# Turning operands on TensorE by halves of 64 rows, and log sums in quarters of the array, in a fused gated recurrence and mixer

## The chip, the core and the metric

The kernel runs on one core of a Trainium2 chip. The metric is device time in microseconds, the median of several executions: 465.51 us for the kernel before the change, from 465.46 to 466.96 over 3 runs. The core has TensorE (matrix products into the eight accumulation banks, PSUM), VectorE, ScalarE, GpSimd, and SyncE, whose queue starts the loads and stores here. In the profile these are PE (with PEld for its weight loads), DVE, ACT, POOL and SP.

## The reference

All data is float32. First a gated linear recurrence is run for each of 4 batches and 8 heads, over 768 time steps with 48 channels; then a mixer works on each batch, a matrix of 768 times by 384 (8 heads of 48).

```python
f = 1.0 / (1.0 + np.exp(-f_logit))
state = np.zeros((B, H, D, D))
for t in range(S):
    state = f[:, :, t, :, None] * state + np.einsum('bhd,bhe->bhde', k[:, :, t], v[:, :, t])
    y[:, :, t] = np.einsum('bhd,bhde->bhe', q[:, :, t], state)
...
h = xt @ U @ V                       # xt: (batch, 384, 768); U: 768 x 32; V: 32 x 768
u = x + h.transpose(0, 2, 1)
out = u + np.maximum(u @ w_ch1, 0.0) @ w_ch2     # 384 -> 1536 -> 384
```

The weights of the mixer arrive as 64-bit floats, and the kernel turns them into 32-bit ones itself.

## The kernel before

**Units.** The recurrence is done in units: one unit is a pair of heads of one batch, so there are 16 units, 4 for each batch. In a unit the 768 steps are 12 chunks of 64 steps (`C = 64`, `NCH = 12`), or 6 blocks of 128 (`NBL = 6`). The channels of the two heads lie on the 128 partitions, each padded from 48 to 64. Inside a chunk the recurrence becomes matrix products: with X, the inverse of the product of the gates from the chunk's end back, and Y, the product from the start on, the scores are (k X)ᵀ (q Y), masked to be causal; between chunks a state of 48 by 48 is carried by a scan.

**Operands.** Loads bring f, k and q with time on the partitions (`nat`), while the products need the channels there (`T["k"]`, which is `kz`, and `T["q"]`, which is `qT`). So TensorE turns each block of 128 times by 128 channels against an identity matrix (`on_tensor`, line 777; for q in units 1 to 3 line 793). VectorE then multiplies the turned block with X or Y, from PSUM into SBUF (lines 799 and 796). Units 0 to 5 do it like this (`TURNED = 6`); later units are turned by VectorE and are not touched.

**Log sums.** In units 0 to 3 X and Y come from logarithms. ScalarE computes log(1 + exp(-f)) (lines 818, 820 and 825). TensorE multiplies each block with a triangular matrix, `later`, 128 by 130: two triangles of 64 on its diagonal, zeros elsewhere, and two more columns that give the sum over each chunk (`log_sums`, line 835). Such a float32 product runs as two passes, a turn as one. ScalarE takes exp of both signs (X and Y, lines 852 and 854), of the whole-chunk sums (`least`, line 856), copies those into a small tile (`wholes`, line 857) and spreads that over the 48 channels for the scan (`whole`, line 1012). Units 4 and 5 use a sigmoid and scans instead (`gates`, `keep`, `read`).

**The rest of a unit.** `scores` (line 975) and `mask` (line 988, VectorE, into `A`), `kept` (line 1002: k turned back, by halves of 64 rows already; then ScalarE's copy `kb`), `states` (line 1026: the increment `ds` of the state; then ScalarE's copy `added`), `scan` (line 1051, VectorE), `read` (line 1069: q times the old state), `inner` (line 1087: the masked scores times v; then ScalarE's copy into `x`). `scores`, `read`, `inner` and `states` already work on 64 rows and 64 columns of the array at a time.

**Order.** For batch 0 and the first mixer the order of every engine is written by hand, by the order of the calls (from line 1180 on). Each engine takes its instructions strictly in that order. In batch 0 nothing but the four units runs, and a unit's front (loads, logs, k, q of unit n + 1) is interleaved with the rear of unit n. VectorE unpacks the loaded k and q of unit n + 1 (line 808) ahead of unit n's scan. SyncE's queue holds the loads of units 0 to 3, U and V, the first weights, and then the loads of units 4 and on. The weights are converted by ScalarE (lines 91 and 92), VectorE (lines 98 to 100) and GpSimd (line 101) through two buffers `w_y`; U and V come at the end of batch 0, ahead of and between the work of unit 3.

Behind batch 0 the mixer of batch 0 starts: `x` is multiplied with U and V, the result is added, x is turned (line 288, by halves of 64 rows), and the first product with `w_ch1` runs (`ch1`, lines 300 and 318, 128 by 128 weights and 256 columns). Units 4 to 7 are interleaved with it, so that each operand of units 4 and 5 is turned between groups of that product. Behind it come the second product (line 355) and the next batches in the same manner, up to the last mixers, which run without units beside them.

**PSUM.** Two pools: `ps_big`, three tiles of two banks, and `ps_mm`, two tiles of one bank. The 128 by 384 matmuls named `idle` (`busy`, line 1190) run at the start, when TensorE has nothing to do yet; one more of 128 columns stands in unit 0.

## Time and profile before

| What | us |
|---|---|
| median of the 3 runs (lowest, highest) | 465.51 (465.46, 466.96) |
| span of the profiled execution, first to last instruction | 463.2 |
| TensorE busy | 455.2 |
| VectorE busy | 351.4 |
| ScalarE busy | 170.4 |
| GpSimd busy | 48.5 |
| batch 0, its four units, up to the mixer's first long group of products | 0 to 47.4 |
| units 4 and 5 turned, between the mixer's products | 55 to 89 |

The page gives no time of the profiled execution other than its span, which is 2.3 us shorter than the median of the runs. The page lists the busy time of each engine, a chain of work followed back from the last instruction, groups of instructions by line, and the loads. A busy TensorE is not TensorE at its best: matmuls overlap, and their ends are modelled. So for TensorE the distance from one group's start to the next one's is the better measure; the chain of waits gives that as a length. A count of matmuls in the profile is a count of passes.

### The profile page before, as it was taken

Reading aid. Unit: us, or ns where it says so; the run is one execution under the profiler, and the core shown is the slowest. Engines: PE = TensorE matmul, PEld = TensorE weight load, DVE = VectorE, ACT = ScalarE, POOL = GpSimd, SP = SyncE. Lnnn points to the kernel's source line nnn. Section 1 sums busy time; section 2 is a strip of 40 time slices with the busy share of each in tenths; the row PEclk is TensorE's granted clock in tenths of the full one; section 3 lists DMA queues with packets and bytes.
Section 4 is the critical chain, followed back from the end, with each engine's and each line's share of the span. In section 5 each row is a group of like instructions: output and inputs, shape, how many; then the busy total and the mean of one; then the engine's idle time right before and its main releaser. Section 6 shows DMA issues by size and latency. Waiting matters only on the chain.

```text
span 463.2 us, 13016 instructions
## 1 busy us (share of the span) xinstructions
PE 455.2 (98%) x5639; PEld 394.5 (85%) x5639; DVE 351.4 (76%) x585; ACT 170.4 (37%) x323; POOL 48.5 (10%) x56
## 2 busy tenths in 40 slices
PE   8999999999999999999999999999999999999997
PEld 5886888875666578999898888899989999999996
DVE  6778788979999677676765559977797887858652
ACT  6785776562333143323322323451412311212200
POOL 2002445634112001010000000000000000000000
PEclk9999999999999999999999999999999999999999
DMA  9959997577777604504633030100000000000001
GB/s 194 186 139 212 227 217 180 150 119 103 124 113 118 107 18 53 78 1 89 77 52 74 14 61 4 28 3 21 18 1 1 35 1 23 13 1 35 1 36 39
DMA packets 148583, 34.35 MB, mean 74 GB/s; under 512 B 136934, under 2 KB 146982, under 8 KB 148518
## 3 DMA queue, kind: packets, MB, share of 16 engines
q1 hardware_dynamic: 147718, 33.29, 37.1%
q8 instruction: 46, 0.75, 0.7%
q10 hardware_dynamic: 800, 0.15, 0.2%
q14 instruction: 19, 0.16, 0.1%
HBM read 28.70 MB, written 4.72 MB: 72 GB/s over the span
## 4 chain that ended last, share of the span: by engine, by line
PE 80%; DVE 11%; ACT 3%; DMA 2%; issue 2%; SPq 2%; DVEq 0%; ACTq 0%
PE pw L389 27%; PE pz L300 21%; PE pp L495 12%; PE po L355 5%; PE y L1069 2%; PE sc L975 2%; PE ds L1026 2%; PE y L1087 2%; PE pt L1002 1%; SPq L661 1%; DVE late L894 1%; PE pt L777 1%; DVE late L876 1%; PE pt L835 1%; DMA other<-in_f_logit_dram 1%
## 5 line engine op out<-in xcount | busy, mean ns | idle before, releaser
L300 PE MATMUL pz<-uT,w 128*128 128x256 f32 x492 | 111.5, 382 | 0.3
L300 PEld LDWEIGHTS pz<-uT,w 128*128 128x128 f32 x492 | 91.7, 190 | 12.9 <-ACT uT L289 0.6
L389 PE MATMUL pw<-zw,w_raw 128*128 128x192 f32 x216 | 38.0, 329 | 0.0
L389 PE MATMUL pw<-w,z_all 128*128 128x192 f32 x216 | 37.3, 327 | 0.0
L335 ACT ACTIVATE z_all<-pz 128x512 f32<-128x512 f32 x33 | 19.6, 598 | 45.1 <-PE pz L300 44.7
L389 PEld LDWEIGHTS pw<-w,z_all 128*128 128x128 f32 x216 | 35.3, 190 | 0.5
L389 PEld LDWEIGHTS pw<-zw,w_raw 128*128 128x128 f32 x216 | 35.1, 190 | 0.6 <-issue 0.3
L101 POOL TENSOR_TENSOR w<-w_y,w_r 128x384 int32<-128x384 int32 x24 | 31.5, 1311 | 37.0 <-DVE w_y L100 22.5
L876 DVE TENSOR_TENSOR_SCAN late<-fz,late 128x768 f32<-128x768 f32 x12 | 21.1, 1755 | 9.4 <-ACT fz L871 9.3
L488 ACT ACTIVATE other<-other 128x512 f32<-128x512 f32 x18 | 11.3, 630 | 40.3 <-DVE other L204 40.3
L355 PE MATMUL po<-w,zw 128*128 128x384 f32 x72 | 25.2, 495 | 0.0
L355 PE MATMUL po<-w,z_all 128*128 128x384 f32 x72 | 24.7, 493 | 0.0
L1057 POOL COPY st<-added 128x576 f32<-128x576 f32 x8 | 12.4, 1556 | 113.8 <-DVE added L1051 113.8
L988 DVE TENSOR_TENSOR A<-sc,causal 128x768 f32<-128x768 f32 x16 | 15.2, 953 | 8.5 <-PE sc L975 8.5
L355 PEld LDWEIGHTS po<-w,zw 128*128 128x128 f32 x72 | 13.2, 190 | 9.6 <-issue 0.8
L894 DVE TENSOR_TENSOR_SCAN late<-fz,other 128x768 f32<-128x768 f32 x12 | 21.0, 1750 | 0.2
L355 PEld LDWEIGHTS po<-w,z_all 128*128 128x128 f32 x72 | 13.3, 190 | 8.9 <-DVE o L204 0.6
L488 ACT ACTIVATE z_all<-z_all 128x512 f32<-128x512 f32 x12 | 7.6, 631 | 34.1 <-DVE z_all L204 34.1
L1034 ACT COPY added<-ds 48x576 f32<-48x576 f32 (+2 forms) x29 | 17.8, 619 | 4.5 <-PE ds L1026 4.1
L495 PE MATMUL pp<-v_nat,late 128*128 128x128 f32 x152 | 19.1, 275 | 0.0
L1069 PEld LDWEIGHTS y<-st,qT 48*64 48x64 f32 x704 | 13.6, 137 | 6.2 <-issue 4.5
L98 DVE TENSOR_SCALAR w_y<-w_y 128x384 f32<-128x384 f32 (+3 forms) x27 | 12.1, 449 | 8.8 <-ACT w_y L91 8.8
(233 smaller groups left out, 872.1 us busy)
## 6 DMA issues: line engine op xcount, KB each, us to landing
w_raw<-in_moe_w_ch_dram SPq DMA_DIRECT2D x18, 384.0 KB, 3.6
out_dram<-o SPq DMA_DIRECT2D x17, 192.0 KB, 1.9
v_nat<-in_v_dram SPq DMA_DIRECT2D x16, 144.0 KB, 3.8
v_nat<-in_v_dram SPq DMA_DIRECT2D x32, 72.0 KB, 3.5
zw<-in_moe_w_ch_dram SPq DMA_DIRECT2D x6, 384.0 KB, 5.1
out_dram<-o SPq DMA_DIRECT2D x14, 96.0 KB, 2.2
w<-in_k_dram SPq DMA_DIRECT2D x4, 288.0 KB, 4.1
w<-in_q_dram SPq DMA_DIRECT2D x4, 288.0 KB, 4.2
```

The costliest lines, as they stand in the source:

```text
L101: nc.gpsimd.tensor_tensor(dst.bitcast(I32), shaped(y.bitcast(I32)), shaped(r), ALU.add)
L300: nc.tensor.matmul(pm[:, i * 2 * P : (i + 1) * 2 * P], lhsT=w1[:, m, o : o + P], rhs=uT[a][:, m, :], start=(m == 0), stop=(m == NDC - 1))
L335: nc.scalar.activation(z[a, c][:, k : k + 2, :].rearrange("p i t -> p (i t)"), pm, AF.Relu)
L355: nc.tensor.matmul(pm, lhsT=z[a, i // NI][:, i % NI, s * P : (s + 1) * P], rhs=w2[:, i, :], start=(i == 0), stop=(i == NFC - 1))
L389: nc.tensor.matmul(W["pm"][:, n * HM : (n + 1) * HM], lhsT=lhs[:, i, :], rhs=rhs[:, i, :], start=(i == 0), stop=(i == NI - 1))
L488: nc.scalar.activation(dst, dst, AF.Relu, scale=float(SIGNS[n]))
L495: nc.tensor.matmul(pm[:, i, r * P : (r + 1) * P], lhsT=room["w"](wn)[:, r * P : (r + 1) * P], rhs=x_node(a, xn), start=((xn, wn) == of[0]) ...
L876: nc.vector.tensor_tensor_scan(backwards(X, S - 1, S), backwards(f, S, S), backwards(ends, S - 1, S), 0.0, ALU.mult, ALU.add,)
L894: nc.vector.tensor_tensor_scan(Y, f[:, 0:S], starts, 0.0, ALU.mult, ALU.add)
L988: nc.vector.tensor_tensor(T["A"], sc[:, :, 0 : NBL * C].rearrange("p h (c i) -> p h c i", i=C), causal.unsqueeze(1).unsqueeze(1).broadcast ...
L1034: nc.scalar.copy(added[r, 1:].rearrange("p (e c s) -> p e c s", c=NBL, s=2)[:, e], ds[r, :, 0 : NBL * D].rearrange("p s (c e) -> p e c s", ...
L1069: nc.tensor.matmul(o(c % 2, par, c // 2), lhsT=T["q"][rows[par], chunk[c]], rhs=T["st"][rows[par], c, :], start=(c <= 2), stop=False, skip ...
```

## The change

1. **Turning by halves.** `on_tensor` (f, k and q of units 0 to 5) and the turn of q in units 0 to 3 take blocks of 64 times by 128 channels: 12 instead of 6 for an operand. The upper and the lower 64 rows go to two different PSUM banks. The turn of q in unit 0 takes two tiles of `ps_mm`, as units 1 to 3 did.
2. **Log sums in quarters.** `later` shrinks to 128 by 65: the triangle of 64 and one column of ones, once for the upper and once for the lower rows. Each block's product becomes four of 64 rows by 64 columns of the array, 65 columns wide, 24 in all instead of 6. In unit 0 the two halves of the blocks go to two tiles of `ps_big`.
3. **Around it.** The views of X, Y, k and q run over halves, then blocks, in place of blocks by threes. The copy of the chunk sums (`wholes`) falls away in units 0 to 3: `spread` reads `least` directly. `whole` becomes a fixed tile whose first column is set once. The `idle` matmul of 128 columns in unit 0 is gone, and so are four small memsets on VectorE at the start and one on GpSimd.

```diff
-    later = const.tile([P, P + 2], F32, name="later")
-    nc.vector.memset(later, 0.0)
+    later = const.tile([P, C + 1], F32, name="later")
+    nc.vector.memset(later, 1.0)
     for s in range(2):
-        half = later[s * C : (s + 1) * C, s * C : (s + 1) * C]
-        nc.vector.memset(half, 1.0)
-        nc.vector.memset(later[s * C : (s + 1) * C, P + s : P + s + 1], 1.0)
+        half = later[s * C : (s + 1) * C, 0:C]
...
         def on_tensor(nm):
 
             pt = ps_big.tile([P, 2, 512], F32, name="pt", tag="big")
+            turn_by_halves(nm, [pt[:, s] for s in range(2)])
+            return pt[:, :, 0 : G * C].rearrange("p s (c t) -> p s c t", t=C)
+
+        def turn_by_halves(nm, pts):
             for c in range(NBL):
-                nc.tensor.transpose(
-                    pt[:, 2 * c // NBL, c % (NBL // 2) * P : (c % (NBL // 2) + 1) * P],
-                    nat[n % 2][nm][:, c].rearrange("p h d -> p (h d)"), ident,
-                )
-            return pt[:, :, 0 : G * C].rearrange("p a (c t) -> p a c t", t=C)
+                for s in range(2):
+                    g = slice(s * C, (s + 1) * C)
+                    nc.tensor.transpose(pts[s][:, c * C : (c + 1) * C],
+                                        nat[n % 2][nm][g, c].rearrange("p h d -> p (h d)"), ident[g, g])
...
-            if nm == "q" and 0 < n < HP:
-                for a in range(2):
-                    pt = ps_mm.tile([P, 512], F32, name="pq", tag="mm")
...
+            if nm == "q" and n < HP:
+                pts = [ps_mm.tile([P, 512], F32, name="pq", tag="mm") for _ in range(2)]
+                turn_by_halves(nm, pts)
+                for s, pt in enumerate(pts):
...
         def log_sums():
...
+            n_of = NBL // 2 if n == 0 else NBL
+            T["sums"] = []
+            for c0 in range(0, NBL, n_of):
+                pt = ps_big.tile([P, 2, 512], F32, name="pt", tag="big")
+                for c in range(n_of):
+                    for i in range(2):
+                        for par in range(2):
+                            k = i ^ par
+                            nc.tensor.matmul(
+                                pt[par * PAD : (par + 1) * PAD, k, c * (C + 1) : (c + 1) * (C + 1)],
+                                lhsT=nat[n % 2]["f"][k * C : (k + 1) * C, c0 + c, par, :],
+                                rhs=later[k * C : (k + 1) * C, :], start=True, stop=True,
+                            )
...
-            nc.scalar.copy(wholes[n % 2][:, 1:NCH], least[:, n, 1:NCH])
+            T["wholes"] = least[:, n, :]
...
         def spread():
-            whole = T["whole"] = one.tile([P, D, NCH], F32, name="whole")
-            nc.scalar.copy(whole, wholes[n % 2].unsqueeze(1).broadcast_to((P, D, NCH)))
+            nc.scalar.copy(whole[:, :, 1:], T["wholes"][:, 1:].unsqueeze(1).broadcast_to((P, D, NCH - 1)))
...
-                pieces += [lambda: busy(1, P)] + front(1, "gates", "gates_end") + rear(0, "scores", "mask")
+                pieces += front(1, "gates", "gates_end") + rear(0, "scores", "mask")
```

On TensorE one period of batch 0, from the increment `ds` of unit 1 to that of unit 2, stands like this before the change (`pt<-later` are the log sums, `pt<-ident,late` k turned, `pq` q turned, `pt<-ident,kz` k turned back; the shape is that of one output):

```order
L1026 MATMUL ds<-v_nat,kb 64x48 x24
L835 MATMUL pt<-later,late 128x130 x6
L975 MATMUL sc<-qT,kz_131 64x64 x24
L777 MATMUL pt<-ident,late 128x128 x6
L1069 MATMUL y<-st,qT 64x48 x22
L793 MATMUL pq<-ident,late 128x128 x6
L1002 MATMUL pt<-ident,kz_130 128x64 x12
L1087 MATMUL y<-v_nat,A 64x48 x24
```

The same period of the changed kernel:

```order
L1022 MATMUL ds<-v_nat,kb 64x48 x24
L834 MATMUL pt<-later,late 64x65 x24
L972 MATMUL sc<-qT,kz_127 64x64 x24
L781 MATMUL pt<-ident,late 128x64 x12
L1065 MATMUL y<-st,qT 64x48 x22
L781 MATMUL pq<-ident,late 128x64 x12
L999 MATMUL pt<-ident,kz_126 128x64 x12
L1083 MATMUL y<-v_nat,A 64x48 x24
```

No group has moved; three of the eight have more and smaller matmuls, and none of the period uses the whole array any more.

VectorE at the end of batch 0 in the changed kernel, from the unpacking of unit 3's k and q (`other<-w_90`) to the conversion of U; the scan is unit 2's:

```order
L806 COPY other<-w_90 128x12x48 x2
L1047 SCALAR_TENSOR_TENSOR st<-added,whole 128x576
L985 TENSOR_TENSOR A<-sc,causal 128x768
L797 TENSOR_TENSOR kz_127<-pt,late 128x768
L98 TENSOR_SCALAR w_y<-w_y 128x192
L99 TENSOR_SCALAR w_y<-w_y 128x192
L100 SCALAR_TENSOR_TENSOR w_y<-w_raw,w_y 128x192
L795 TENSOR_TENSOR qT<-pq,fz_125 128x384 x2
```

Before the change the same place reads (with the old line numbers):

```order
L808 COPY other<-w_90 128x12x48 x2
L1051 SCALAR_TENSOR_TENSOR st<-added,whole 128x576
L988 TENSOR_TENSOR A<-sc,causal 128x768
L799 TENSOR_TENSOR kz_131<-pt,late 128x768
L98 TENSOR_SCALAR w_y<-w_y 128x192
L99 TENSOR_SCALAR w_y<-w_y 128x192
L100 SCALAR_TENSOR_TENSOR w_y<-w_raw,w_y 128x192
L796 TENSOR_TENSOR qT<-pq,fz_129 128x128x3 x2
```

The order is the same; only the two multiplications of q run over halves of 64 times in place of blocks by threes. SyncE's loads stand in the same order before and after. On the mixer's side, each `L777 ... 128x128 x6` between groups of `L300` of units 4 and 5 has become `L781 ... 128x64 x12` at the same place.

## The prediction

> **What bounds the kernel now.** I read the page first, then the chain of waits in order of time, then the waits of each engine, and last the timelines of VectorE, ScalarE and SyncE where the chain leaves TensorE.

> ```profile
> PE 455.2 (98%) x5639; PEld 394.5 (85%) x5639; DVE 351.4 (76%) x585; ACT 170.4 (37%) x323; POOL 48.5 (10%) x56
> ```

> TensorE is busy 455.2 us of the span of 463.2, so at first sight every microsecond taken from it counts. The page has no time of the profiled execution beside this span; the median of the runs is 465.5 us, 2.3 us more. I work out a difference in the span and take it off the median.

> The change touches two stretches. In the first, the four units of batch 0, the chain runs along TensorE, unit after unit:

> ```profile
> 18.22 1.54 PE pt L835 x12
> 19.75 0.86 PE sc L975 x48
> 20.61 0.81 PE pt L777 x6
> ...
> 21.43 1.24 PE y L1069 x41
> 22.67 0.81 PE pq L793 x6
> 23.48 0.54 PE pt L1002 x12
> ...
> 24.89 0.92 PE ds L1026 x48
> ```

> Columns: start, length, engine and line, count. This is one unit: log sums (6 matmuls in two passes each), scores, k turned, old state read, q turned, k turned back. Only L1002 already goes by 64 rows: its 12 half blocks take 0.54, where 6 whole blocks take 0.81. But the next engine is close behind, as a window of one unit's length shows (length, then busy of PE, PEld, DVE, ACT, POOL):

> ```profile
> 15.80:23.40 7.60, 7.54 (x225) 6.57 (x224) 5.52 (x9) 6.24 (x14) 0.00 (x0) 1.00 0.94 213
> ```

> ScalarE has 6.24 of 7.60 us, VectorE 5.52, and the share of the DMA engines is 0.94. The second stretch, units 4 and 5, lies in 55 to 89 us, between the mixer's matmuls:

> ```profile
> 67.08 0.66 PE pt L777 x6
> 67.73 2.59 PE pz L300 x12
> 70.33 0.52 PE pt L1002 x12
> 70.84 2.79 PE pz L300 x12
> ```

> **The change, step by step: batch 0 on TensorE.** Each k or q turned by halves goes from 0.81 to L1002's 0.54: 0.27 less, twice a unit. The log sums become 24 matmuls, 48 passes, of 64 rows, 64 columns and 65 moving columns, on four quarters. No row has that shape. Nearest are the scores, also 48 passes on quarters with 64 moving columns (48 rows):

> ```profile
> 185.48 0.71 PE sc L975 x48
> 186.19 0.52 PE pt L1002 x12
> ```

> Here, with half-array work behind them, they take 0.71, and 0.86 above where whole-array work follows. For the log sums I take 0.80; the bounds are 0.71 and the 1.54 of now (no overlap gained). So they give 0.74, the two turns 0.54, the scores 0.15: 1.4 us of TensorE per unit.

> [...]

> **What of it reaches the end of batch 0.** Unit 0 gives nothing: its kz stands on VectorE behind the unpacking of its q, which waits for the load until 6.72:

> ```profile
> 6.72 0.46 DVE L808 COPY late<-w 128x576 f32<-128x576 f32 x1 [0.53 <-DMA w<-in_q_dram]
> ```

> Unit 1's log sums start when ScalarE's second half of the logs is done, as now:

> ```profile
> 11.66 1.61 PE L835 MATMUL pt<-later,other 128*128 128x130 f32 x12 [0.23 <-ACT other L825]
> ```

> From there ScalarE goes 0.7 earlier, and unit 1's `ds` (the matmuls of the state's increment) with it. Unit 2 adds its 0.74 and 0.15, so its `ds` (24.89) comes about 1.6 earlier. The copies of L857 (0.20 each on ScalarE) that fall away are part of what lets ScalarE follow. Then VectorE meets a load:

> ```profile
> 25.05 0.46 DVE L808 COPY other<-w 128x576 f32<-128x576 f32 x1 [0.76 <-DMA w<-in_k_dram]
> 26.19 0.46 DVE L808 COPY other<-w 128x576 f32<-128x576 f32 x1 [0.69 <-DMA w<-in_q_dram]
> 26.57 1.35 DVE L1051 TENSOR_TENSOR_SCAN st<-added,whole 128x576 f32<-128x576 f32 x1
> 28.56 0.96 DVE L988 TENSOR_TENSOR A<-sc,causal 128x768 f32<-128x768 f32 x1 [0.64 <-PE sc L975]
> 29.44 0.95 DVE L799 TENSOR_TENSOR kz<-pt,late 128x768 f32<-128x768 f32 x1
> ...
> 31.53 1.04 DVE L796 TENSOR_TENSOR qT<-pq,fz 128x384 f32<-128x384 f32 x2 [0.29 <-PE pq L793]
> ...
> 34.13 1.41 DVE L1051 TENSOR_TENSOR_SCAN st<-added,whole 128x288 f32<-128x288 f32 x2 [0.85 <-ACT added L1034]
> ```

> VectorE takes its work in order, and the unpacking of unit 3's k and q (L808) stands ahead of unit 2's scan, before and after. q lands at 26.19. Today that wait costs nothing, since the scan's input `added` comes from ScalarE at 26.51 (25.87 + 0.64 below). After the change it is there 1.6 earlier, and the scan still starts at 26.57. Will q land earlier? SyncE issues it from a queue with no pause:

> ```profile
> 20.34 0.55 SPq L640 DMA_DIRECT2D w<-in_k_dram  x1
> 20.93 0.47 SPq L640 DMA_DIRECT2D w<-in_q_dram  x1
> ```

> SyncE's waits name no compute engine between 17 and 20 us, the order of loads is the same after the change, and the DMA share is 0.94. I take the landing as fixed; the bounds are 0.4 later and, if TensorE or ScalarE do gate it, early enough not to bind.

> So at 26.57 everything gained so far is gone on VectorE, and what comes back is the idle time behind it. The scan ends at 27.92. The mask A follows at once instead of at 28.56, so kz of unit 3 is 0.64 earlier and ends at 29.75; TensorE, ahead by then, waits for the scan, reads the state (1.24), turns q (0.54) and turns k back at 29.8 instead of 31.30, 1.5 earlier. The conversion of U (L98 to L100, left out above) is 0.64 earlier too, and the wait of 0.29 for pq goes. ScalarE and GpSimd at this place:

> ```profile
> 25.87 0.64 ACT L1034 COPY added<-ds 128x576 f32<-128x576 f32 x1
> ...
> 31.39 0.59 POOL L101 TENSOR_TENSOR U<-w_y,w_r 128x192 int32<-128x192 int32 x1 [27.29 <-DVE w_y L100]
> ...
> 31.86 0.80 ACT L1006 COPY kb<-pt 128x768 f32<-128x768 f32 x1 [0.72 <-PE pt L1002]
> 32.56 0.32 ACT L91 ACTIVATE w_y<-w_raw 64x128 f32<-64x128 f32 x1
> ...
> 33.70 0.70 ACT L1034 COPY added<-ds 128x288 f32<-128x288 f32 x2
> ```

> The L91 at 32.56 writes the buffer (one of two) that GpSimd's add for U reads until 31.39 + 0.59 = 31.98; that becomes 31.34, so this L91 moves 1.2, not 1.5, and `added` and the last scan (34.13, whose 0.85 of idle covers it) move 1.2 with it. From that scan to 41.9 us the chain runs on VectorE almost without idle and hands this on to the mixer's start at 47.4. **Batch 0 gives 1.2 us**; bounds 0 and 2.7. The 2.7 is what arrives if no load binds: 1.6 up to `ds` of unit 2, and 0.74 + 0.15 + 0.27 of unit 3's log sums, scores and k.

> **Units 4 and 5.** Here whole-array matmuls of the mixer stand on both sides. Six whole blocks take 0.66 with 2.59 behind them; the half blocks of L1002 take 0.52, but the 12 passes of L300 behind them take 2.79 instead of 2.59. Together 3.25 against 3.31: **each turn by halves loses 0.06**, where a view of L1002 alone promises 0.14. Five of the six (f, k, q, f, k) come before 86 us: 0.3 lost. This part is PE's own path:

> ```profile
> 47.40:86.20 38.80, 38.80 (x249) 33.84 (x248) 33.90 (x60) 27.11 (x53) 18.39 (x16) 1.00 0.87 202
> 86.20:134.10 47.90, 47.11 (x775) 33.21 (x775) 42.65 (x59) 21.00 (x41) 15.38 (x10) 1.00 0.75 119
> ```

> [...]

> From 86 to 134 us the chain runs along VectorE (42.65 of 47.90 busy) and the loads that it frees, and TensorE then waits:

> ```profile
> PE pt L1002 <- DVE kz L805: 0.2, 1, 0.2
> ```

> That chain begins at a matmul's end at 86.2, so it moves as a whole with TensorE; the sixth turn (0.06) has this 0.2 as cover. Behind 134 us nothing changes.

> Removed memsets, the idle matmul of unit 0 and the narrower copy into `whole` lie beside waits: nothing, at most 0.1 each way. **Sum: 1.2 - 0.3 = 0.9 us less, 464.6 us** (span 462.3).

> **Rivals.**
> - *No load binds.* TensorE's gain of batch 0 passes on: 2.7 - 0.3 = 2.4, 463.1 us. For it: TensorE at 98%. Against it: the 0.69 wait for q at 26.19, with the scan 0.08 behind it.
> - *The gain is given back.* The loop of weight conversion and loads from 47 to 134 us, VectorE 33.90 of 38.80 and then 42.65 of 47.90 busy, does not start earlier, and only the six dearer turns stay: 465.5, at worst 465.9. Against it: its head hangs on TensorE and ScalarE, with waits between 47 and 86.
> - *The clock drops: slower.* TensorE's first matmuls, at the kernel's start, run at half rate although the clock column says 1.00:

> ```profile
> 1.07 4.09 PE L1190 MATMUL idle<-late 128*128 128x384 f32 x6 [1.07 <-DVE late L667]
> ...
> 98.62 4.03 PE L355 MATMUL po<-w,z_all 128*128 128x384 f32 x12
> ```

> Six passes of 384 columns take 4.09 there, twelve take 4.03 later. After the change TensorE idles about 1.7 us before 28 us, waiting for the scan, longer than any wait now (the longest is 1.1, at the start). If that is enough to slow it, 4.1 us of its work run at half rate and cost 2.05, just where it is on the path: 464.6 + 2.1 = 466.7. [...]

> **How the numbers follow.** Forecast (0.3 to 1.4 less) 0.58; no load binds 0.19; given back 0.17; clock 0.06. A measurement tells about 0.3%, 1.4 us, from no change. The forecast lies inside that. Faster by more: the first rival and the forecast's edge, 0.22; slower by more: part of the clock rival and worse drains, 0.06; same 0.72. The range goes from 463.0 (no load binds) to 466.0 (given back at its worst, 465.9) and leaves out the clock rival and the thin ends.

> **What would show it.** Right: log sums of 48 passes near 0.8 us and turns near 0.54 in batch 0; VectorE still waiting for q at 26.2, now with TensorE idle until the scan ends near 28; the first L300 group near 46.2 instead of 47.4; twelve passes of L300 at 2.8 behind every turn of units 4 and 5. Wrong: a scan of unit 2 well before 26.5, log sums above 1.0, or the six turns saving time.

## The result, and the profile after

The changed kernel takes **477.75 us**, the median of 4 runs (476.85 to 478.32), against 466.07 for the kernel before on the same chip (465.46 to 466.96): a ratio of 1.0247, 95% interval 1.0227 to 1.0267. (The ratios in this document are estimates, each with its interval, and not the quotients of the medians.) The forecast was 464.6, its range 463.0 to 466.0. The profiled execution has a span of 475.1 us, 11.9 more than before.

The page of the changed kernel, first the busy time of TensorE, then the queue that carries instructions (packets, MB, share):

```profile
PE 458.7 (97%) x5865; PEld 395.1 (83%) x5865; DVE 350.6 (74%) x582; ACT 169.6 (36%) x319; POOL 48.5 (10%) x55
...
q8 instruction: 48, 0.79, 0.7%
```

TensorE is busy 3.5 us longer, though the groups were to get shorter. The second line will matter: 0.79 MB in 48 packets are 16.4 KB each, for 2 x 5865 weight loads and matmuls about 245 instructions to a packet.

The chain of waits in time (start, length, what) shows where the time goes:

```profile
11.36 0.73 PE pt L834 x33
12.10 2.11 issue
14.21 0.46 PE pt L834 x15
14.67 0.52 PE pt L781 x12
...
20.36 0.66 PE pt L834 x42
...
21.30 2.05 issue
23.35 0.73 PE sc L972 x33
24.09 0.52 PE pt L781 x12
...
37.88 0.46 PE sc L972 x26
38.34 1.97 issue
40.31 0.57 PE sc L972 x19
...
43.59 0.82 PE y L1083 x43
44.42 2.21 issue
46.63 0.45 PE y L1083 x5
...
52.65 2.00 PE pz L318 x4
...
58.98 3.22 PE pz L300 x14
```

Where it isn't interrupted, the changed work takes what was forecast: log sums of 48 passes about 0.75 (42 in 0.66), turns 0.52. But TensorE stops four times for 2 us **inside** a group, with "issue": it waits for nothing that the profile shows. All operands of such a group are there, since its first 26 or 33 passes ran. The first long group of L300 starts at 58.98. In the chain of the kernel before the same groups stand at:

```profile
42.95 1.06 PE pz L318 x4
...
47.44 7.97 PE pz L300 x36
```

So 11.5 of the 11.9 us are lost by then. TensorE's waits up to 60 us in the changed kernel (total, times, longest) put a number on it:

```profile
PE sc L972 <- issue: 4.0, 2, 2.0
PE y L1083 <- issue: 2.8, 3, 2.2
PE pt L834 <- issue: 2.1, 1, 2.1
```

Together 8.9 us; before the change the same view has one such row:

```profile
PE y L1069 <- issue: 0.4, 1, 0.4
```

The second loss is the clock. Windows (start:end, length, busy of PE and PEld, DVE, ACT, POOL; then the granted clock):

```profile
12.20:15.60 3.40, 1.39 (x51) 1.25 (x54) 1.45 (x3) 0.85 (x2) 0.00 (x0) 1.00 0.85 170
15.60:19.00 3.40, 3.38 (x88) 3.09 (x81) 2.92 (x6) 3.03 (x7) 0.00 (x0) 0.50 1.05 213
...
42.90:46.30 3.40, 1.52 (x47) 1.01 (x45) 2.92 (x5) 1.47 (x4) 1.49 (x3) 1.00 1.19 279
46.30:56.60 10.30, 9.97 (x67) 6.40 (x67) 3.61 (x7) 2.97 (x7) 0.76 (x1) 0.50 0.80 187
```

Behind three of the four long stalls the granted clock falls to half. These stretches last 3.4, 6.8 and 10.2 us, 20.5 us in all; before the change there is none. Behind the stall at 38.34 the clock stays full. What half rate means stands in the chain: four passes of L318 take 2.00 at 52.65, and took 1.06 before.

**What the stalls have in common is a number.** The same view with borders put into the stalls, for the changed kernel; the counts in brackets behind PE and PEld are matmuls and weight loads:

```profile
0.00:13.00 13.00, 9.67 (x219) 6.60 (x220) 8.55 (x19) 8.06 (x16) 3.19 (x20) 1.00 1.01 196
13.00:18.90 5.90, 4.69 (x127) 4.34 (x127) 3.47 (x8) 3.78 (x8) 0.00 (x0) 0.72 0.91 196
18.90:22.00 3.10, 2.17 (x131) 1.95 (x126) 1.17 (x2) 2.59 (x5) 0.00 (x0) 0.98 0.67 134
22.00:28.00 6.00, 4.41 (x127) 3.87 (x127) 4.03 (x8) 3.02 (x7) 0.00 (x0) 0.82 0.65 166
28.00:39.00 11.00, 9.94 (x380) 9.16 (x381) 6.55 (x13) 8.05 (x23) 1.05 (x2) 0.79 0.27 83
39.00:45.50 6.50, 4.11 (x127) 2.96 (x126) 5.15 (x12) 2.58 (x7) 1.44 (x2) 1.00 0.92 270
```

From stall to stall it is 254 or 257 matmuls and loads, or three times as many (761). With TensorE's other instructions counted, every gap falls behind instruction 449, 705, 961 and on, exactly 256 apart, close to the 245 instructions of a packet. The table lists each border for the profiled executions: how long TensorE worked on the block of 256 ahead of it, and how long it then waited, counted from the start of the block's last instruction to the start of the next one (the view of waits counts from the end of a matmul, so its sum is smaller).

| border | before: block, wait | after: block, wait | after: from the block's start to the next one's |
|---|---|---|---|
| 449 | 5.60, 0.00 | 2.76, 2.33 | 5.09 |
| 705 | 3.79, 0.00 | 4.47, 0.53 | 5.00 |
| 961 | 4.40, 0.00 | 1.88, 2.27 | 4.14 |
| 1217 | 3.64, 0.23 | 4.11, 0.68 | 4.79 |
| 1473 | 4.63, 0.00 | 3.39, 0.24 | 3.64 |
| 1729 | 3.31, 0.68 | 3.94, 0.00 | 3.94 |
| 1985 | 6.81, 0.31 | 2.40, 2.19 | 4.59 |
| 2241 | 21.25, 0.21 | 3.89, 2.43 | 6.32 |

In the kernel before, the 0.31 and the 0.21 at the last two borders are no waits for a block: they stand behind matmuls of 256 columns, which start 0.2 us or more apart there anyway (12 in 2.59). Where TensorE had to wait in the changed kernel, the next block was there 3.6 to 6.3 us after the current one was begun. A unit of batch 0 has 448 TensorE instructions before (a matmul of two passes is four, a turn of one pass is two) and 544 after, and of the new ones the 96 of the log sums go through in about 0.75 us, so a block is now through in as little as 1.9 us. The kernel before was already at this edge: up to border 1729 its blocks take 3.3 to 5.6 us, and it waits 0.23 and 0.68 us.

### The profile page after: what moved, and what is told of

It reads as the page before. It is cut to its first block, busy times and chain, and to the rows that moved or that the text cites. A ratio compares the mean times of both kernels' runs of the same rounds, so it can differ in the third digit from the quotient of the medians.

```text
span 475.1 us, 13465 instructions
## 1 busy us (share of the span) xinstructions
PE 458.7 (97%) x5865; PEld 395.1 (83%) x5865; DVE 350.6 (74%) x582; ACT 169.6 (36%) x319; POOL 48.5 (10%) x55
## 4 chain that ended last, share of the span: by engine, by line
PE 83%; DVE 8%; issue 3%; ACT 2%; DMA 2%; SPq 1%; DVEq 0%
PE pw L389 26%; PE pz L300 23%; PE pp L495 12%; PE po L355 5%; PE y L1083 3%; PE y L1065 3%; PE sc L972 2%; PE ds L1022 2%; PE pt L999 2%; DMA other<-in_f_logit_dram 1%; PE pz L318 1%; PE put L288 1%; PE pt L781 1%; DMA w<-in_q_dram 1%; PE ph L184 1%
## 5 line engine op out<-in xcount | busy, mean ns | idle before, releaser
L300 PE MATMUL pz<-uT,w 128*128 128x256 f32 x492 | 112.1, 383 | 0.3 <-ACT uT L289 0.2
L300 PEld LDWEIGHTS pz<-uT,w 128*128 128x128 f32 x492 | 91.7, 190 | 13.3 <-ACT uT L289 0.6
L101 POOL TENSOR_TENSOR w<-w_y,w_r 128x384 int32<-128x384 int32 x24 | 31.4, 1310 | 43.4 <-DVE w_y L100 24.3
L488 ACT ACTIVATE other<-other 128x512 f32<-128x512 f32 x18 | 11.3, 631 | 40.3 <-DVE other L204 40.3
L355 PE MATMUL po<-w,zw 128*128 128x384 f32 x72 | 25.2, 495 | 0.0
L355 PE MATMUL po<-w,z_all 128*128 128x384 f32 x72 | 24.7, 493 | 0.0
L355 PEld LDWEIGHTS po<-w,zw 128*128 128x128 f32 x72 | 13.2, 190 | 9.6 <-issue 0.8
L1083 PEld LDWEIGHTS y<-v_nat,A 64*64 64x64 f32 x768 | 14.4, 143 | 7.6 <-issue 6.6
L355 PEld LDWEIGHTS po<-w,z_all 128*128 128x128 f32 x72 | 13.3, 190 | 8.9 <-DVE o L204 0.6
L98 DVE TENSOR_SCALAR w_y<-w_y 128x384 f32<-128x384 f32 (+3 forms) x27 | 11.9, 441 | 10.9 <-ACT w_y L91 10.9
L1083 PE MATMUL y<-v_nat,A 64*64 64x48 f32 x768 | 16.8, 231 | 2.8 <-issue 2.8
```

Source lines behind the costliest of these rows:

```text
L101: nc.gpsimd.tensor_tensor(dst.bitcast(I32), shaped(y.bitcast(I32)), shaped(r), ALU.add)
L300: nc.tensor.matmul(pm[:, i * 2 * P : (i + 1) * 2 * P], lhsT=w1[:, m, o : o + P], rhs=uT[a][:, m, :], start=(m == 0), stop=(m == NDC - 1))
L355: nc.tensor.matmul(pm, lhsT=z[a, i // NI][:, i % NI, s * P : (s + 1) * P], rhs=w2[:, i, :], start=(i == 0), stop=(i == NFC - 1))
L488: nc.scalar.activation(dst, dst, AF.Relu, scale=float(SIGNS[n]))
L1083: nc.tensor.matmul(o(s, par, c), lhsT=T["A"][part[s ^ par], par, c, :], rhs=vt[part[s ^ par], c, par, :], start=False, stop=True, skip_gro ...
```

## The experiments

Two theories went into the first four runs. **A**: instructions in blocks of 256 arrive late once TensorE is too fast for them, and a stall costs clock as well. **B**: the changed shapes themselves stall TensorE (halves and quarters of the array next to whole ones). In all four the kernel before measured 466.72 us (13 runs).

**Halves in units 4 and 5 only.**

```diff
             pt = ps_big.tile([P, 2, 512], F32, name="pt", tag="big")
+            if n >= HP:
+                turn_by_halves(nm, [pt[:, s] for s in range(2)])
+                return pt[:, :, 0 : G * C].rearrange("p s (c t) -> p s c t", t=C)
```

> Before, with f, k and q of units 4 and 5 alone turned by halves. Theory A (TensorE runs out of instructions in batch 0, because these are fetched in blocks of 256 and the smaller matmuls use them up faster than blocks arrive): no stall here, since the mixer's matmuls around these turns take 0.2 us each; the six turns cost 0.06 us each, so 0.3 to 0.4 us slower than before, clock 1.00 throughout. Theory B (the half and quarter shapes themselves stall TensorE): stalls of about 2 us at these turns too, several us slower.

466.79 us, ratio 1.0006 (0.9991 to 1.0021). No stall stands at the six turns. One of 1.6 us stands in batch 0, where nothing was changed, at instruction 961: how near the edge the kernel before runs. The 0.3 us forecast for these turns is inside the interval.

**Turns by halves in units 0 to 3 only** (472 instructions in a unit).

```diff
             pt = ps_big.tile([P, 2, 512], F32, name="pt", tag="big")
+            if n < HP:
+                turn_by_halves(nm, [pt[:, s] for s in range(2)])
...
-                for a in range(2):
-                    pt = ps_mm.tile([P, 512], F32, name="pq", tag="mm")
...
+                pts = [ps_mm.tile([P, 512], F32, name="pq", tag="mm") for _ in range(2)]
+                turn_by_halves(nm, pts)
```

> Before, with k and q of units 0 to 3 alone turned by halves; 24 more TensorE instructions (loads of weights and matmuls) in a unit, 472 instead of 448. Theory A: TensorE would need 7.0 us for a unit, blocks of 256 at about 4.1 us each allow 7.6, so stalls of at most 0.5 us that begin at whole multiples of 256 instructions from the first one (instruction 449 of TensorE, 705, 961 and so on); time within 1 us of before unless a stall lets the clock drop. Theory B (quarters of the log sums alone stall): no stall, 0.5 to 1 us faster.

471.90 us (468.49 to 474.26), ratio 1.0126 (1.0098 to 1.0154). In the profiled execution gaps of 1.53, 1.10, 1.97 and 1.26 us stand at 705, 961, 1729 and 1985. A was right on the place and too low on the size: 24 instructions more in a unit cost 5 us. The four executions of this one program show how the time goes with the clock:

```
time (us)   mean clock
468.49      1.000
471.65      0.992
472.14      0.985
474.26      0.977
```

At 0.977 about 21.7 us run at half rate (2 x 0.023 of the span of 472.4), and the time is 5.8 us longer than at full clock: some 0.27 us for each. The execution at 0.992 gives 0.42 in the same way, so 0.27 is a rough estimate; the stalls, too, may differ between executions.

**Log sums in quarters only** (520 instructions), and **by halves of 64 rows with all 128 columns** (472).

```diff
+                    for i in range(2):
+                        for par in range(2):
+                            k = i ^ par
...
+                                lhsT=nat[n % 2]["f"][k * C : (k + 1) * C, c0 + c, par, :],
```

```diff
+                    for k in range(2):
+                        nc.tensor.matmul(
+                            pt[:, k, c * (C + 1) : (c + 1) * (C + 1)],
+                            lhsT=nat[n % 2]["f"][k * C : (k + 1) * C, c0 + c].rearrange("p h d -> p (h d)"),
```

> Before, with the log sums of units 0 to 3 in quarters and all turns of whole blocks; 72 more TensorE instructions in a unit, 520 instead of 448. Theory A: stalls of 1 us or more at multiples of 256 instructions as in the changed kernel, though they now fall into other groups of matmuls than there; half clock behind the longest ones; 470 to 477 us. Theory B: stalls inside the log sums in every unit, wherever the 256 fall.

> The log sums by halves of 64 rows and all 128 columns of the array (12 matmuls, 24 more instructions in a unit, 472), all turns of whole blocks. Theory A: as turns_only, TensorE needs about 6.9 us for a unit and gets its instructions in 7.6, stalls of at most 0.7 us at multiples of 256; time within 1 us of before unless the clock drops. Theory B (quarters stall): no stall, 0.5 to 1 us faster than before.

472.08 us, ratio 1.0119 (1.0089 to 1.0150), and 472.90, 1.0150 (1.0116 to 1.0183). Again the gaps stand at the borders (2.75 at 449 and 2.01 at 961; 1.51, 1.71 and 1.22 at 705, 1729 and 1985), in a different group each time. The quarters came out in A's range of 470 to 477; for the halves A's limit of 1 us was too low again. In that kernel an undisturbed group of log sums (24 passes, at 29.94 us) takes 1.49 us, where whole ones take 1.54: this shape gains next to nothing for its 24 instructions. B falls with these four: the stalls don't follow the shapes. The next two turn the question round.

**The kernel before, only with more instructions.**

```diff
+                for j in range(1 if b else 2):
+                    w = C if b else C // 2
...
+                                sc[part[s ^ par], par, c * C + j * w : c * C + (j + 1) * w],
```

> The kernel before, none of the change in it; only the 24 scores matmuls of each unit of batch 0 are 48, with 32 instead of 64 moving columns: 544 TensorE instructions in a unit, as many as after the change, and the same arithmetic. Theory A (TensorE's instructions come in blocks of 256 and arrive late when a unit issues more of them): stalls in which the profile shows no reason at the boundaries 449, 705, 961 and so on, together 5 us or more over batch 0, some half clock, and a time 5 to 12 us over before. Theory B (the changed shapes, halves and quarters of the array next to whole ones, are what stalls TensorE): no stall over 0.7 us, and at most 2 us over before, for the 192 extra loads of weights in each of four units.

479.27 us, ratio 1.0289 (1.0241 to 1.0337): as slow as the changed kernel, with no part of the change in it. It is 12.9 us over the kernel before, which measured 466.38 (13 runs) beside this run and the next three; A had said 5 to 12. The gaps, 1.25, 1.74, 1.73 and 3.06 us, stand at 449, 705, 1985 and 2241. Its windows, borders put into the stalls, show the same counts:

```profile
0.00:15.20 15.20, 12.75 (x219) 9.94 (x219) 9.92 (x24) 9.90 (x20) 3.16 (x21) 1.00 1.02 194
15.20:20.50 5.30, 3.75 (x127) 3.14 (x127) 2.44 (x6) 3.65 (x9) 0.00 (x0) 1.00 1.12 199
20.50:41.50 21.00, 19.43 (x633) 17.48 (x634) 12.25 (x21) 13.53 (x33) 1.05 (x2) 0.92 0.36 96
41.50:48.00 6.50, 4.00 (x127) 2.87 (x126) 4.91 (x11) 1.89 (x6) 1.44 (x2) 1.00 1.07 289
```

**The change, with fewer instructions.** In each unit of batch 0 the 24 scores matmuls of 64 columns become 12 of 128, and 20 of the 24 masked products with v are left out.

```diff
+                    if b == 0:
+                        nc.tensor.matmul(
+                            sc[:, par, c * C : (c + 1) * C],
+                            lhsT=T["k"][rows[par], 2 * c * C : (2 * c + 2) * C],
...
-            for c in reversed(range(NBL)):
+            for c in reversed(range(NBL if b else 1)):
```

> The changed kernel with all of its halves and quarters, but in batch 0 the scores go by 12 matmuls of 128 instead of 24 of 64 columns, and of the masked products with v only those of the first block are left (4 of 24): 416 TensorE instructions in a unit instead of 544, and y of batch 0 is not the reference's. Theory A: stalls together under 2.5 us over batch 0, clock full throughout, the mixer's first long group between 45 and 48.5 us instead of 59, and a time of 463 to 468. Theory B: the stalls stay, together 6 us or more, with half clock, and the time stays above 472.

477.36 us, ratio 1.0234 (1.0209 to 1.0259). A's stalls came out (2.5 us in all), its time didn't. One stall was left, at 449, and the chain and the windows of this kernel show what it did:

```profile
12.54 0.46 PE pt L781 x9
13.00 2.01 issue
15.01 0.28 PE pt L781 x2
...
22.06 2.75 PE sc L972 x24
```

```profile
15.00:30.00 15.00, 13.95 (x315) 12.77 (x319) 8.38 (x14) 8.02 (x15) 0.00 (x0) 0.54 0.71 166
30.00:45.00 15.00, 14.50 (x280) 12.82 (x272) 8.34 (x16) 7.87 (x22) 1.05 (x2) 0.50 0.30 96
45.00:60.00 15.00, 14.82 (x134) 9.61 (x131) 7.59 (x20) 5.40 (x13) 3.44 (x4) 0.50 1.08 234
```

Half rate from 16.2 to 60.5 us, 44 us behind a single stall, though TensorE is busy 93 to 99% of that time. The other four executions of this kernel have a mean clock of 0.957, some 41 us at half rate, so it was no accident of one. So A needs its second half, and the price of a stall is not its length.

**Fewer loads.** The loads of k, q and v of units 1 to 3 are left out, in the changed kernel and in the one before.

```diff
+            if 0 < n < HP and nm in "kqv":
...
+                continue
```

> The changed kernel without the loads of k, q and v of units 1 to 3 (unit 0's are used again, so that y of batch 0 is not the reference's). If blocks of instructions are late because their transfer waits behind loads: the stalls near 12 and 21 us shrink below 1 us each, those behind 30 us, where weights are loaded earlier than now, may stay or move; less half clock than 20.5 us in all, and at most 1.5% over the kernel before with the same loads left out. If the time of such a transfer has nothing to do with loads: stalls of 2 us at the same instruction numbers, and 2 to 3% over that kernel.

> The kernel before without the loads of k, q and v of units 1 to 3, as the one to compare with: VectorE no longer waits for loads at 25 and 26 us, 0 to 3 us less than before, no stall over 0.7 us.

473.25 us, ratio 1.0161 (1.0121 to 1.0202), and 465.44, 0.9985 (0.9975 to 0.9994). Loads delay the blocks, but are not the whole of it. The first block now follows 3.80 us after the one ahead of it was begun, instead of 5.09; its packet starts at 10.63, 1.2 us after that, where it started 2.0 after with the loads. From a packet's start to the first instruction of its block it is 2.3 to 3.1 us in both. Between 15 and 28 us, at a DMA share of 0.2, stalls of 1.60 and 1.50 stay: late blocks still come 3.6 to 3.8 us after the one ahead was begun, about 14.5 ns for an instruction. (The least for a late block in any run was 3.0, once, in the kernel with quarters only; and the kernel before without these loads went on after 3.3 us with no wait at border 1729. So it is no fixed price.) At that, 544 of them need 7.9 us; a unit took 7.6 before. Half rate lasted 10.2 us instead of 20.5. So of the first expectation only the half rate came out: the stalls near 12 and 20 us went down to 1.0 and 1.6, not below 1, and the kernel is 1.7% over its partner, not 1.5 at most. Nor did they stay at 2 us, as the second had it.

**Both cut**, in the changed kernel (416 instructions in a unit) and in the one before (320): the cuts of the last two experiments together.

> The changed kernel with both: 416 TensorE instructions in a unit of batch 0 (12 scores matmuls of 128 columns, 4 of 24 masked products with v) and no loads of k, q and v in units 1 to 3; y of batch 0 is not the reference's. Theory C (a block of 256 instructions is there 3.6 to 3.8 us after the block ahead of it was begun when few loads run, 4.1 to 6.3 us when many do; TensorE stalls for what it is faster; and one stall of 2 us is enough for half clock): no stall over 0.7 us, clock full throughout, and a time of 460 to 466. Rival (the half clock of 44 us in the kernel with fewer instructions came from its scores of 128 columns, not from its stall of 2.2 us): half clock for 10 us or more again, and 470 or more.

> The kernel before with the same work left out (320 TensorE instructions in a unit of batch 0), as the one to compare with: 460 to 466. If the change gains what was forecast as soon as instructions are no limit, the changed kernel with the same left out is 0.3 to 1.5 us faster than this one; if the gain wasn't there at all, they are equal or this one is faster.

463.80 us, ratio 0.9950 (0.9934 to 0.9966), and 467.38, 1.0041 (1.0012 to 1.0069), against 466.41 (18 runs) for the kernel before. Freed of the limit, **the changed kernel is the faster by 3.6 us**. The chain gives the increments `ds` of units 1 and 2 and the mixer's first groups, here of the changed kernel:

```profile
17.35 0.92 PE ds L1036 x48
...
24.16 0.91 PE ds L1036 x48
...
41.09 1.06 PE pz L318 x4
...
45.58 7.97 PE pz L300 x36
```

and here of the kernel before with the same cuts:

```profile
17.90 0.92 PE ds L1040 x48
...
20.35 1.49 PE sc L981 x24
...
26.03 0.91 PE ds L1040 x48
...
44.38 1.06 PE pz L318 x4
...
48.87 7.97 PE pz L300 x36
```

3.3 us earlier. From one `ds` to the next it is 6.81 against 8.13 us: 1.32 less, close to the 0.74 and 0.54 that the prediction had for log sums and turns of a unit. The gain as a whole is over twice the 0.3 to 1.5 us expected, and this pair favours the change: no late load of k and q holds VectorE, and the scores of this shape take 1.49 us where the usual 48 passes take 0.86, so that the partner's chain stays on TensorE longer. That goes with another miss, the partner being a little slower than the kernel before without cuts. The changed kernel is 2.6 us below that one.

The rival of this turn falls: the changed kernel has the same scores of 128 columns and the same matmuls as the one with half rate for 44 us, but no long stall, and half rate for 3.4 us only. Even these were not expected: they came behind a window with no such stall, in which TensorE was busy 0.72 of the time.

**The change without most masked products** (4 of 24 kept, all loads, scores as usual; 464 instructions).

```diff
-            for c in reversed(range(NBL)):
+            for c in reversed(range(NBL if b else 1)):
```

> The changed kernel with its usual scores and all loads, but only 4 of the 24 masked products with v in a unit of batch 0: 464 TensorE instructions in a unit; y of batch 0 is not the reference's. Theory C: the first block is as late as in the changed kernel (stall of about 2 us at instruction 449), the later ones less, together 3 to 7 us; half clock behind the first stall, and 468 to 478. If the long half clock of the kernel with fewer instructions came from its stall and its light load together, it lasts over 15 us here too; if from its scores of 128 columns, at most 10 us.

471.12 us (469.11 to 474.75), ratio 1.0121 (1.0063 to 1.0178). As theory C had it, the first block is late by 2.34 us, as in the changed kernel, and all gaps sum to 3.6 us. Half rate lasts 10.2 us behind the first stall and 6.8 later. That is between the two expectations, so why half rate lasted 44 us in the other kernel stays open: its scores of 128 columns may be part of it together with the stall, but not by themselves, as the kernel with both cuts shows.

## Why the prediction was wrong

**The failing step is "batch 0 on TensorE".** It priced the added matmuls by the time that the array takes for them ("For the log sums I take 0.80"), and took 24 matmuls in place of 6 to cost nothing beyond it. The array times were right; what was missing is a second limit, instructions per time. In place of a gain the runs showed a unit's 544 instructions used up faster than their blocks of 256 came: 8.9 us of stalls, and 20.5 us at half rate behind them. The trace of before had the rows for it: 448 instructions in a unit of 7.6 us, 17 ns each, against the 96 instructions that a group of scores issues in 0.71 to 0.86 us, 7 to 9 ns each. With the gaps of 0.23 and 0.68 us at two of the borders, the nearness of the edge could have been read there. I passed over the one row with "issue" as the cause (0.4 at L1069).

**Point by point.**

- *Log sums at 0.80, turns at 0.54, 1.4 us a unit:* log sums and turns right where nothing interrupts (0.75 and 0.52 at full clock). For the scores' 0.15, units 1 to 3 of the changed kernel have no undisturbed group at full clock.
- *Batch 0 gives 1.2 us, bounds 0 and 2.7:* wrong by sign, since it loses 11.5. With instructions and loads no limit, 3.3 us arrive at the mixer, somewhat over the upper bound (with other work cut too, and in a pair that favours the change, so not the same case).
- *VectorE waits for q at 26.2 us:* it never came to that. Unit 3's k and q are unpacked at 27.55 without a wait, since TensorE is late already. The load of q, issued at 20.71, took 4.7 us and landed at 25.4, so the landing at 26.19 that was taken as fixed moved too. What an undisturbed kernel with all its loads would have gained, no run shows.
- *Units 4 and 5, each turn dearer by 0.06:* right. The "worse drains" in the chances no run shows; the runs showed this 0.06 in their place. The chain of the changed kernel has, between two turns, 24 passes behind each at 5.38, where it was 0.66 and 5.18:

```profile
66.94 0.52 PE pt L781 x12
67.46 5.38 PE pz L300 x24
72.84 0.52 PE pt L781 x12
73.35 5.38 PE pz L300 x24
```

- From the first L300 to the scores behind the last turn it is 47.52 us (58.98 to 106.50) against 47.11 (47.44 to 94.55): 0.4 more, 0.3 to 0.36 forecast.
- *The clock rival:* its effect came, for five times as long, and by another cause. It saw TensorE wait for a scan; what made TensorE idle was the missing block. Its price of 2.05 stood for 4.1 us at half rate; there were 20.5. Its chance of 0.06 was an estimate that no run shows.
- *The sum:* 8.5 us more of stalls (8.9 less 0.4) and 20.5 us at half rate with 0.27 each, 5.5, less a gain of 2.7 to 3.3, are 10.7 to 11.3, against 11.5 measured. The 0.27 is a rough figure from another kernel of this case, so the split between stalls and clock is an estimate.

**What is shown and what isn't.** That the loss is one of instructions and not of shapes is shown from both sides: the kernel before with split scores loses as much, and the changed kernel with fewer instructions and loads gains. That the first packet starts later beside loads is shown by the pair with and without them (2.0 against 1.2 us); what holds it back, no run shows. How the time of 2.3 to 3.1 us between a packet's start and its use is made up, no run shows. Nor is it shown why half rate lasts as long as it does. No version that computes everything and beats the kernel before came out of this: its own blocks have hardly any room left.

## What to carry to other kernels

Count instructions, not only array time: each pass is a weight load and a matmul, two instructions (5865 of each in the changed kernel), and here a late block of 256 came 3.6 to 3.8 us after the one ahead was begun with few loads (3.0 once), and up to 6.8 us with many (the kernel before with split scores). As an estimate from these rows, some 15 to 20 ns an instruction on the average of a block is what this kernel could be fed at; by that estimate splitting its matmuls for the array's quarters would have paid where a stretch stays above it. "Issue" waits inside a group, 256 instructions or a multiple of it apart, were the sign of it here, and the small one before the change (0.4) was a warning.
